# Folding the even columns of a 1024-point real transform once more on VectorE, forward and inverse

## The chip, the cores and the metric

The kernel runs on one core of one Trainium2 chip. Its time is the device time of that core in microseconds (us); lower is better, and a median over several runs is quoted. "Span" is the length of the one profiled execution.

A round is a series in which several kernels and the kernel before run in turn on one chip. The kernel before had a median of 1442.5 us (3 runs) when the prediction was made, 1442.78 us beside the changed kernel, and 1444.96, 1441.37 and 1440.81 us in the three rounds of experiments.

## The reference, cut to what matters

```python
def _A_ref(x, w_r, w_i):                    # the spectral branch
    X = jnp.fft.rfft2(x.astype(jnp.float32), axes=(-2, -1))
    X = X * (w_r + 1j * w_i)
    return jnp.fft.irfft2(X, s=(S, D), axes=(-2, -1)).astype(jnp.bfloat16)

def _B_ref(x, w1, b1, w2, b2):              # the dense branch: squared ReLU
    h = jnp.einsum("bsd,df->bsf", x, w1) + b1
    r = jnp.where(h > 0, h, 0)
    return jnp.einsum("bsf,fd->bsd", r * r, w2) + b2

g = sigmoid((x * gate_w).sum(-1, keepdims=True))
out = g * _A_ref(x, ...) + (1 - g) * _B_ref(x, ...)
# returned: out and, for a given grad_out, the gradients of all inputs of the two branches
# S = 2048, D = 1024, F = 3584, everything bfloat16
```

For output and gradient the kernel needs two real 2D transforms forward (of `x` and of the gated gradient) and two back. Each consists of 16 row tiles of 128 rows, so there are 32 forward and 32 inverse tiles. The change concerns the transform along D = 1024 inside each tile.

## The kernel before

TensorE does the dense branch in matmuls of 512 columns. Transform tiles are woven into that stream by generators: `spread` runs a step of the transform after a given number of dense steps. A forward tile is folded on VectorE, goes through eight 128-column matmuls (the part of the transform along S inside the tile, called "blocks" below), is copied to SBUF by ScalarE (`ft`), goes through eight matmuls against constant tables (the "column stage"), and is copied out of PSUM by ScalarE (`u`), with even and odd outputs interleaved.

```python
def one_s1(fb, cf, T, i, xt, kmat):                  # a forward tile
    ...                                              # uv: sum and difference of the two halves
    f = fb.tile([P, 4, Q], FDT, name="f", tag="f", bufs=2)
    a0, a1 = uv[:, :, 1:Q], uv[:, :, H - 1 : Q : -1]
    V(out=f[:, 0:2, 1:Q], in0=a0, in1=a1, op=ALU.add)
    V(out=f[:, 2:4, 1:Q], in0=a0, in1=a1, op=ALU.subtract)
    ...                                              # two small copies for the edge elements
    pk = fps.tile([P, 8, P], FP32, name="pk", tag="ps2", bufs=2)
    fl = f[:].rearrange("p a b -> p (a b)")
    for b in range(8):                               # the blocks
        mm(pk[:, b, :], lhsT=fl[:, b * P : (b + 1) * P], rhs=kmat, start=True, stop=True)
    ft = fb.tile([P, 8, P], FDT, name="ft", tag="ft", bufs=2)
    nc.scalar.copy(out=ft[:], in_=pk[:])
    pu = fps.tile([P, 2, H], FP32, name="pu", tag="ps2", bufs=2)
    column_stage(FWD, pu, ft, cf)                    # 512+257+257+255 and 4x256 columns
    u = fb.tile([P, H, 2], FDT, name="u", tag="u", bufs=2)
    nc.any.tensor_copy(out=u[:].rearrange("p j b -> p b j"), in_=pu[:])
    st(out=z_scr[T][:]..., in_=u[:]...)

FWD = (
    (4, 0, 0, H, 1), (0, 0, 0, Q + 1, 0), (1, 0, 0, Q + 1, 0), (5, 0, Q + 1, Q - 1, 2),
    (6, 1, 0, Q, 1), (7, 1, 0, Q, 2), (2, 1, Q, Q, 1), (3, 1, Q, Q, 2),
)
...
def mlp_in():                                        # the dense stage beside the forward tiles
    ...
            ph = mps.tile([P, SW], FP32, name="ph", tag="ph", bufs=2)
            for dc in range(DC):                     # eight matmuls of 512 columns
                mm(ph[:], lhsT=w1g[:, dc, fs], rhs=xT[:, dc, ss], start=(dc == 0), stop=(dc == DC - 1))
            rT = wb.tile([P, SW], BF16, name="rT", tag="rT", bufs=3)
            nc.scalar.activation(rT[:], ph[:], ACT.Relu, bias=b1col[:, fc : fc + 1])
            nc.scalar.activation(h2T[:, ss], rT[:], ACT.Square)
            pd = mps.tile([P, SW], FP32, name="pd", tag="ph", bufs=2)
            for ec in range(DC):                     # eight more
                mm(pd[:], lhsT=w2T[f2][:, ec, :], rhs=dbT[:, ec, ss], start=(ec == 0), stop=(ec == DC - 1))
            STT(out=dhT[:, ss], in0=pd[:], scalar=2.0, in1=rT[:], op0=ALU.mult, op1=ALU.mult, ...)
    ...
def fft_out():                                       # the inverse tiles
    ...
            for b in range(8):
                par, q4 = divmod(b, 4)
                mm(pk[:, b, :], lhsT=r[:, q4 * P : (q4 + 1) * P, par], rhs=ki[:], start=True, stop=True)
            rt = ...                                 # ScalarE copy, as ft above
            column_stage(INV, pu, rt, ci)
            e = fb.tile([P, 2, H], FDT, name="e", tag="e", bufs=2)
            nc.scalar.copy(out=e[:], in_=pu[:])
            ...                                      # VectorE unfolds e, result to DRAM
```

`ph` and `pd` share a tag with two buffers. So the eight matmuls of the next `ph` cannot start before the ReLU `rT` has read the last one, and ScalarE does the ReLU in order, behind the copies of the transform tile.

## Time and profile before

| | kernel before |
|---|---|
| time, median of 3 runs | 1442.5 us (1440.09 to 1443.06) |
| span of the profiled run | 1438.6 us |
| forward tiles (32) | about 83 to 433 us, beside `ph` and `pd` |
| inverse tiles (32) | about 890 to 1134 us, beside the weight gradients and the output |
| `u` copy on ScalarE, 128x1024, written at step 2 | 1304 ns |

The lines on which the bound was read stand in the prediction below. Here is one steady forward tile in the timeline of the kernel before, TensorE and ScalarE alone. The columns are start (us), duration (us), engine, line, operation, output and inputs, tile and count, and in brackets the idle time before it with what ended it.

```profile
214.33 1.17 PE L267 MATMUL pu<-cf,ft 128*128 128x512 f16 x8
...
215.34 1.24 PE L583 MATMUL ph<-xT,w1g 128*128 128x512 bf16 x5
215.54 1.31 ACT L251 CAST u<-pu 128x1024 f16<-128x1024 f32 x1 [1.07 <-PE pu L267]
...
216.42 1.89 PE L591 MATMUL pd<-dbT,w2T 128*128 128x512 bf16 x8
216.71 0.69 ACT L585 ACTIVATE rT<-ph,b1col 128x512 bf16<-128x512 f32 x1
...
218.15 1.89 PE L583 MATMUL ph<-xT,w1g 128*128 128x512 bf16 x8
```

TensorE finishes the column stage, then five matmuls of `ph`, then eight of `pd`. Meanwhile ScalarE copies `u` and then does the ReLU. The 218.15 at which TensorE writes the ReLU's buffer again is the pace of an unbroken stream: 216.42 + 8 x 0.216 = 218.15.

### The profile page before, as it was taken

The numbers are of one execution on the slowest core, as the hardware profiler recorded it, in microseconds if no ns is written. First come the engines' busy times: TensorE is split into PE (matmuls) and PEld (weight loads), VectorE is DVE, ScalarE is ACT, GpSimd is POOL, SyncE is SP. The second block draws the span as 40 slices with busy tenths as digits, with TensorE's granted clock in tenths as the row PEclk, the third lists the DMA queues.
The fourth block names the chain that finished last, engine by engine and source line by source line (L and its number), as shares of the span: only waits on it lengthen the run. The fifth ranks groups of instructions, "written<-read, shape, count | busy, mean of one in ns | idle before, by whom it ended". The sixth has DMA issues, their size and how long they took to land. (4 is left out here: it accounts for less than half of the span.)

```text
span 1438.6 us, 19451 instructions
## 1 busy us (share of the span) xinstructions
PE 1394.8 (97%) x7562; PEld 674.0 (47%) x7562; DVE 674.9 (47%) x1303; ACT 420.0 (29%) x590; POOL 299.3 (21%) x483
## 2 busy tenths in 40 slices
PE   6689999999999999999999999999999999999997
PEld 4455555555554444444444444445554444444443
DVE  2564554455444466445554534113566555652222
ACT  4245555555553322222232222334322100000000
POOL 0012222222223333333442122111110000000000
PEclk9899999999999999999999999999999999999999
DMA  7476766666669967998977678777557647563530
GB/s 234 128 235 205 218 193 204 223 216 205 191 183 255 257 200 201 187 229 189 220 146 187 143 132 188 221 205 231 194 198 228 210 147 221 177 187 96 146 95 22
DMA packets 220214, 271.57 MB, mean 189 GB/s; under 512 B 16077, under 2 KB 153307, under 8 KB 220123
## 3 DMA queue, kind: packets, MB, share of 16 engines
q1 hardware_dynamic: 184122, 151.80, 39.9%
q0 software_dynamic: 36000, 118.54, 27.9%
q8 instruction: 59, 0.97, 0.3%
q14 instruction: 33, 0.26, 0.1%
HBM read 151.77 MB, written 118.51 MB: 188 GB/s over the span
## 5 line engine op out<-in xcount | busy, mean ns | idle before, releaser
L583 PE MATMUL ph<-xT,w1g 128*128 128x512 bf16 x896 | 218.6, 382 | 1.4 <-ACT xT L493 0.9
L591 PE MATMUL pd<-dbT,w2T 128*128 128x512 bf16 x896 | 215.3, 383 | 1.6 <-DVE dbT L493 1.6
L692 PE MATMUL pw<-grp,res 128*128 128x512 bf16 x896 | 209.6, 387 | 0.0
L675 PE MATMUL pw<-dbn,grp 128*128 128x512 bf16 x896 | 198.0, 379 | 1.5 <-DVE row L639 1.5
L753 PE MATMUL acc<-w,hblk 128*128 128x512 bf16 x896 | 198.6, 379 | 0.0
L794 PE MATMUL accg<-w1Tr,hblk 128*128 128x512 bf16 x896 | 193.5, 379 | 0.0
L591 PEld LDWEIGHTS <-w2T 128*128 128x128 bf16 x896 | 87.4, 99 | 109.1 <-issue 5.1
L585 ACT ACTIVATE rT<-ph,b1col 128x512 bf16<-128x512 f32 x112 | 77.0, 688 | 207.9 <-PE ph L583 159.7
L794 PEld LDWEIGHTS <-hblk 128*128 128x128 bf16 x896 | 87.7, 98 | 105.7
L675 PEld LDWEIGHTS <-grp 128*128 128x128 bf16 x896 | 87.1, 98 | 105.8 <-issue 2.4
L692 PEld LDWEIGHTS <-res 128*128 128x128 bf16 x896 | 85.0, 96 | 109.0
L753 PEld LDWEIGHTS <-hblk 128*128 128x128 bf16 x896 | 87.0, 98 | 98.6
L583 PEld LDWEIGHTS <-w1g 128*128 128x128 bf16 x896 | 85.3, 98 | 86.6 <-issue 4.5
L592 DVE SCALAR_TENSOR_TENSOR dhT<-pd,rT 128x512 bf16<-128x512 f32 x112 | 75.3, 673 | 104.5 <-PE pd L591 60.9
L604 DVE STREAM_TRANSPOSE stg<-h2T 128x512 int32<-128x512 int32 x56 | 39.8, 711 | 130.2 <-ACT h2T L586 130.2
L679 ACT CAST wo<-pw 128x512 bf16<-128x512 f32 x56 | 32.8, 586 | 165.7 <-PE pw L675 152.3
L697 ACT CAST wo<-pw 128x512 bf16<-128x512 f32 x56 | 32.9, 587 | 142.0 <-PE pw L692 132.2
L687 POOL DMA_DIRECT2D out_dram<-wo x112 | 56.3, 516 | 81.9 <-ACT wo L679 61.4
L795 DVE TENSOR_TENSOR gxo<-accg,g 128x512 bf16<-128x512 f32 x32 | 22.1, 691 | 107.6 <-PE accg L794 107.4
L306 DVE CAST x<-px 128x1024 f16<-128x1024 f32 x16 | 19.6, 1224 | 111.5 <-PE px L305 111.5
L461 DVE TENSOR_TENSOR tt<-e 128x512 f16<-128x512 f16 x32 | 13.6, 425 | 124.2 <-ACT e L459 123.5
L586 ACT ACTIVATE h2T<-rT 128x512 bf16<-128x512 bf16 x112 | 70.5, 629 | 3.4
(169 smaller groups left out, 1488.6 us busy)
## 6 DMA issues: line engine op xcount, KB each, us to landing
h_scr<-stg POOLq DMA_DIRECT2D x28, 512.0 KB, 6.1
dh_scr<-stg POOLq DMA_DIRECT2D x28, 512.0 KB, 7.4
h2T_scr<-h2T POOLq DMA_DIRECT2D x28, 512.0 KB, 4.9
dhT_scr<-dhT POOLq DMA_DIRECT2D x28, 512.0 KB, 6.6
grp<-h_scr SPq DMA_DIRECT2D x112, 128.0 KB, 5.3
grp<-dh_scr SPq DMA_DIRECT2D x112, 128.0 KB, 4.6
hblk<-h2T_scr SPq DMA_DIRECT2D x8, 1792.0 KB, 9.1
hblk<-dhT_scr SPq DMA_DIRECT2D x8, 1792.0 KB, 8.9
```

The lines of the kernel that those rows point to most:

```text
L583: mm(ph[:], lhsT=w1g[:, dc, fs], rhs=xT[:, dc, ss], start=(dc == 0), stop=(dc == DC - 1))
L585: nc.scalar.activation(rT[:], ph[:], ACT.Relu, bias=b1col[:, fc : fc + 1])
L586: nc.scalar.activation(h2T[:, ss], rT[:], ACT.Square)
L591: mm(pd[:], lhsT=w2T[f2][:, ec, :], rhs=dbT[:, ec, ss], start=(ec == 0), stop=(ec == DC - 1))
L592: STT(out=dhT[:, ss], in0=pd[:], scalar=2.0, in1=rT[:], op0=ALU.mult, op1=ALU.mult, accum_out=gb1part[:, fc, sb : sb + 1],)
L604: nc.vector.transpose(out=stg[k_, sb][:, :, f2, :], in_=src[:, cols2].bitcast(I32).rearrange("p (b i) -> p b i", i=32),)
L675: mm(pw[:], lhsT=cur[:, t // 2, 2 * fb_ * P + t % 2 : 2 * (fb_ + 1) * P : 2], rhs=dbn[:, t, hf * H : (hf + 1) * H], start=(t == 0), stop=( ...
L687: st(out=dst[q], in_=wo[32 * q : 32 * (q + 1), :])
L692: mm(pw[:], lhsT=xr[t][:, d_ * P : (d_ + 1) * P], rhs=cur[:, t // 2, t % 2 :: 2], start=(t == 0), stop=(t == NT - 1),)
L697: nc.scalar.copy(out=wo[:].rearrange("p (q a j) -> p a q j", q=4, j=32), in_=pw[:].rearrange("p (a q j) -> p a q j", q=4, j=32),)
L753: mm(acc[:], lhsT=cur[:, fc, t2::2], rhs=w2[:, fc, cs], start=(fc == 0), stop=(fc == FC - 1))
L794: mm(acc[:], lhsT=cur[:, fc, t2::2], rhs=w1T[:, fc, cs], start=(fc == 0), stop=(fc == FC - 1))
```

## The change

The even-numbered outputs of the transform can be split once more into those divisible by four and the others. For that VectorE forms sums and differences of mirrored halves, forward before the blocks and inverse after the column stage. In exchange the four even matmuls of a column stage shrink from 512, 257, 257 and 255 columns to 256, 129, 128 and 128. In the changed kernel `u` collects four groups of outputs, one for each remainder on division by four, so its copy, which restores the natural order, writes runs of 256 elements at a step of four instead of two. The inverse reads its stationary blocks at a step of four.

```diff
-        f = fb.tile([P, 4, Q], FDT, name="f", tag="f", bufs=2)
+        f = fb.tile([P, 6, Q], FDT, name="f", tag="f", bufs=2)
         ...
+        b0, b1 = f[:, 0:3:2, 1:P], f[:, 0:3:2, Q - 1 : P : -1]
+        V(out=f[:, 4:6, 1:P], in0=b0, in1=b1, op=ALU.add)
+        V(out=f[:, 4:6, P + 1 : Q], in0=b0, in1=b1, op=ALU.subtract)
+        V(out=f[:, 4, 0:1], in0=uv[:, 0, 0:1], in1=uv[:, 0, Q : Q + 1], op=ALU.add)
+        V(out=f[:, 4, P : P + 1], in0=uv[:, 0, 0:1], in1=uv[:, 0, Q : Q + 1], op=ALU.subtract)
+        nc.scalar.copy(out=f[:, 5, P::-P], in_=f[:, 0:3:2, P])
         ...
-        nc.any.tensor_copy(out=u[:].rearrange("p j b -> p b j"), in_=pu[:])
+        nc.any.tensor_copy(
+            out=u[:].rearrange("p (i h) b -> p b h i", h=2), in_=pu[:].rearrange("p b (h i) -> p b h i", h=2)
+        )
         ...
     FWD = (
-        (4, 0, 0, H, 1), (0, 0, 0, Q + 1, 0), (1, 0, 0, Q + 1, 0), (5, 0, Q + 1, Q - 1, 2),
-        (6, 1, 0, Q, 1), (7, 1, 0, Q, 2), (2, 1, Q, Q, 1), (3, 1, Q, Q, 2),
+        (0, 0, 2 * P, 0, 1), (0, 0, P + 1, 0, 2), (0, 2 * P, P, 0, 3), (0, 3 * P, P, 0, 3),
+        (1, 0, 2 * P, P, 1), (1, 0, 2 * P, P, 2), (1, P, 2 * P, P, 1), (1, P, 2 * P, P, 2),
     )
         ...
-                    mm(pk[:, b, :], lhsT=r[:, q4 * P : (q4 + 1) * P, par], rhs=ki[:], start=True, stop=True)
+                    mm(pk[:, b, :], lhsT=rf[:, im * H + l_ : (im + 1) * H : 4], rhs=ki[:], start=True, stop=True)
         ...
+                ev = fb.tile([P, 2, Q], FDT, name="ev", tag="ev", bufs=2)
+                A, B = (e[:, 0, o : o + Q].rearrange("p (c d) -> p c d", c=2) for o in (0, Q))
+                V(out=ev[:, :, 0:P], in0=A, in1=B, op=ALU.add)
+                evf = ev[:].rearrange("p c d -> p (c d)")
+                V(out=evf[:, Q:P:-1], in0=A[:, 0, :], in1=B[:, 0, :], op=ALU.subtract)
+                V(out=evf[:, 2 * Q - 1 : Q + P : -1], in0=B[:, 1, 1:], in1=A[:, 1, 1:], op=ALU.subtract)
+                nc.vector.tensor_copy(out=ev[:, :, P : P + 1], in_=e[:, 0, P::Q].rearrange("p (c o) -> p c o", o=1))
         ... # cut: the constant tables cf and ci in their new order, INV, the unfolding that reads ev
```

More of the change, by code (lines that the diff above doesn't have):

```diff
@@ L64, in build_consts @@
     w = lambda l, d: tp * ((l[None, :] * d[:, None]) % D) / D
-    le, lo = np.arange(0, D // 2 + 1, 2), np.arange(1, D // 2, 2)
-    lei = le[1:-1]
+    l4, l42 = np.arange(0, D // 2 + 1, 4), np.arange(2, D // 2, 4)
+    lo = np.concatenate([np.arange(1, D // 2, 4), np.arange(3, D // 2, 4)])
     d0, d1 = np.arange(P), np.arange(P, 2 * P)
-    dz = d0.copy()
-    dz[0] = Q
-    even = np.zeros((P, 2 * Q))
-    even[:, Q + 1 :] = -np.sin(w(lei, d0))
-    even[0, : Q + 1] = np.cos(w(le, np.array([Q])))[0]
+    dz, dh = d0.copy(), d0.copy()
+    dz[0], dh[0] = Q, P
+    blk_n = np.concatenate([np.zeros((P, P + 1)), -np.sin(w(l4[1:-1], d0))], axis=1)
+    blk_n[0, : P + 1] = np.cos(w(l4, np.array([P])))[0]
     parts = [
-        even,
-        np.cos(w(le, d0)), np.cos(w(le, d1)), -np.sin(w(lei, d1)),
+        blk_n, np.cos(w(l4, d0)), np.cos(w(l42, d0)), -np.sin(w(l42, dh)),
         np.cos(w(lo, d0)), np.cos(w(lo, d1)), -np.sin(w(lo, dz)), -np.sin(w(lo, d1)),
@@ L78, in build_consts @@
     c["cf"] = np.concatenate(parts, axis=1).astype(FDT_NP)
-    de, ds = np.arange(Q + 1), np.arange(1, Q)
+    v = lambda l, d: tp * ((l[:, None] * d[None, :]) % D) / D
+    cof = lambda l: np.where((l == 0) | (l == 2 * Q), 1.0, 2.0)[:, None]
     dq = np.arange(Q)
@@ L83, in build_consts @@
     dzq[0] = Q
-    l0e, l1e = np.arange(0, Q, 2), np.arange(Q, 2 * Q, 2)
-    l0o, l1o = np.arange(1, Q, 2), np.arange(Q + 1, 2 * Q, 2)
-    v = lambda l, d: tp * ((l[:, None] * d[None, :]) % D) / D
-    cof = lambda l: np.where((l == 0) | (l == 2 * Q), 1.0, 2.0)[:, None]
-    ev = np.zeros((P, 2 * Q))
-    ev[1:, Q + 1 :] = -2.0 * np.sin(v(l0e[1:], ds))
-    ev[0, : Q + 1] = np.cos(np.pi * de)
+    m4, m42 = np.arange(0, D // 2, 4), np.arange(2, D // 2, 4)
+    m1, m3 = np.arange(1, D // 2, 4), np.arange(3, D // 2, 4)
+    da = np.arange(P + 1)
+    ev = np.concatenate([np.zeros((P, P + 1)), -2.0 * np.sin(v(m4, da[1:-1]))], axis=1)
+    ev[0] = 0.0
+    ev[0, : P + 1] = np.cos(np.pi * da)
     parts = [
-        ev,
-        cof(l0e) * np.cos(v(l0e, de)), cof(l1e) * np.cos(v(l1e, de)), -2.0 * np.sin(v(l1e, ds)),
-        2.0 * np.cos(v(l0o, dq)), 2.0 * np.cos(v(l1o, dq)), -2.0 * np.sin(v(l0o, dzq)), -2.0 * np.sin(v(l1o, dzq)),
+        ev, cof(m4) * np.cos(v(m4, da)), 2.0 * np.cos(v(m42, d0)), -2.0 * np.sin(v(m42, dh)),
+        2.0 * np.cos(v(m1, dq)), 2.0 * np.cos(v(m3, dq)), -2.0 * np.sin(v(m1, dzq)), -2.0 * np.sin(v(m3, dzq)),
     ]
@@ L239, in one_s1 @@
         V(out=f[:, 2:4, 1:Q], in0=a0, in1=a1, op=ALU.subtract)
-        nc.scalar.copy(out=f[:, 0::3, 0:1], in_=uv[:, :, 0:1])
-        nc.scalar.copy(out=f[:, 2:0:-1, 0:1], in_=uv[:, :, Q : Q + 1])
+        nc.scalar.copy(out=f[:, 3, 0:1], in_=uv[:, 1, 0:1])
+        nc.scalar.copy(out=f[:, 1, 0:1], in_=uv[:, 1, Q : Q + 1])
+        b0, b1 = f[:, 0:3:2, 1:P], f[:, 0:3:2, Q - 1 : P : -1]
[4 more added lines that the diff above has]
+        nc.scalar.copy(out=f[:, 5, P::-P], in_=f[:, 0:3:2, P])
         pk = fps.tile([P, 8, P], FP32, name="pk", tag="ps2", bufs=2)
-        fl = f[:].rearrange("p a b -> p (a b)")
-        for b in range(8):
-            mm(pk[:, b, :], lhsT=fl[:, b * P : (b + 1) * P], rhs=kmat, start=True, stop=True)
+        for b, (row, o) in enumerate(((5, P), (4, 0), (4, P), (5, 0), (3, 0), (3, P), (1, 0), (1, P))):
+            mm(pk[:, b, :], lhsT=f[:, row, o : o + P], rhs=kmat, start=True, stop=True)
         ft = fb.tile([P, 8, P], FDT, name="ft", tag="ft", bufs=2)
@@ L250, in one_s1 @@
         u = fb.tile([P, H, 2], FDT, name="u", tag="u", bufs=2)
-        nc.any.tensor_copy(out=u[:].rearrange("p j b -> p b j"), in_=pu[:])
+        nc.any.tensor_copy(
+            out=u[:].rearrange("p (i h) b -> p b h i", h=2), in_=pu[:].rearrange("p b (h i) -> p b h i", h=2)
+        )
         st(out=z_scr[T][:].rearrange("c (p i) l -> i (c p) l", i=S2)[i], in_=u[:].rearrange("p j b -> p (j b)"))
     FWD = (
-        (4, 0, 0, H, 1), (0, 0, 0, Q + 1, 0), (1, 0, 0, Q + 1, 0), (5, 0, Q + 1, Q - 1, 2),
-        (6, 1, 0, Q, 1), (7, 1, 0, Q, 2), (2, 1, Q, Q, 1), (3, 1, Q, Q, 2),
-    )
-    INV = (
-        (2, 0, 0, H, 1), (0, 0, 0, Q + 1, 0), (1, 0, 0, Q + 1, 0), (3, 0, Q + 1, Q - 1, 2),
-        (4, 1, 0, Q, 1), (5, 1, 0, Q, 2), (6, 1, Q, Q, 1), (7, 1, Q, Q, 2),
-    )
+        (0, 0, 2 * P, 0, 1), (0, 0, P + 1, 0, 2), (0, 2 * P, P, 0, 3), (0, 3 * P, P, 0, 3),
+        (1, 0, 2 * P, P, 1), (1, 0, 2 * P, P, 2), (1, P, 2 * P, P, 1), (1, P, 2 * P, P, 2),
+    )
+    INV = FWD[:4] + ((1, 0, Q, 0, 1), (1, 0, Q, 0, 2), (1, Q, Q, 0, 1), (1, Q, Q, 0, 2))
     def column_stage(table, pu, ft, mat):
         o = 0
-        for (b, bank, lo, n, f_) in table:
+        for b, (bank, lo, n, skip, f_) in enumerate(table):
+            out = pu[:, bank, lo : lo + n]
+            if skip:
+                out = pu[:, bank, :].rearrange("p (h c i) -> p c h i", h=2, c=2)[:, lo // P]
             mm(
-                pu[:, bank, lo : lo + n], lhsT=ft[:, b, :], rhs=mat[:, o : o + n],
+                out, lhsT=ft[:, b, :], rhs=mat[:, o : o + n],
                 start=bool(f_ & 1), stop=bool(f_ & 2), skip_group_check=True,
@@ L450, in fft_out @@
                 pk = fps.tile([P, 8, P], FP32, name="pki", tag="ps2", bufs=2)
-                for b in range(8):
-                    par, q4 = divmod(b, 4)
-                    mm(pk[:, b, :], lhsT=r[:, q4 * P : (q4 + 1) * P, par], rhs=ki[:], start=True, stop=True)
+                rf = r[:].rearrange("p j b -> p (j b)")
+                for b, (im, l_) in enumerate(((1, 0), (0, 0), (0, 2), (1, 2), (0, 1), (0, 3), (1, 1), (1, 3))):
+                    mm(pk[:, b, :], lhsT=rf[:, im * H + l_ : (im + 1) * H : 4], rhs=ki[:], start=True, stop=True)
                 rt = fb.tile([P, 8, P], FDT, name="rt", tag="rt", bufs=2)
@@ L459, in fft_out @@
                 nc.scalar.copy(out=e[:], in_=pu[:])
+                ev = fb.tile([P, 2, Q], FDT, name="ev", tag="ev", bufs=2)
[5 more added lines that the diff above has]
+                nc.vector.tensor_copy(out=ev[:, :, P : P + 1], in_=e[:, 0, P::Q].rearrange("p (c o) -> p c o", o=1))
                 tt = fb.tile([P, 2, 2, Q], FDT, name="tt", tag="tt", bufs=2)
-                V(out=tt[:, 0].rearrange("p a b -> p (a b)"), in0=e[:, 0, :], in1=e[:, 1, :], op=ALU.add)
-                V(out=tt[:, 1].rearrange("p a b -> p (a b)"), in0=e[:, 0, :], in1=e[:, 1, :], op=ALU.subtract)
+                V(out=tt[:, 0].rearrange("p a b -> p (a b)"), in0=evf, in1=e[:, 1, :], op=ALU.add)
+                V(out=tt[:, 1].rearrange("p a b -> p (a b)"), in0=evf, in1=e[:, 1, :], op=ALU.subtract)
                 yo = fb.tile([P, D], FDT, name="yo", tag="yo", bufs=2)
```

## The prediction

> **What bounds the kernel now.** I read the page's busy shares first, then its forty slices, then the windows view by stage, then the timeline of TensorE, and last the groups by line.
>
> ```profile
> PE 1394.8 (97%) x7562; PEld 674.0 (47%) x7562; DVE 674.9 (47%) x1303; ACT 420.0 (29%) x590; POOL 299.3 (21%) x483
> ...
> PE   6689999999999999999999999999999999999997
> ...
> PEclk9899999999999999999999999999999999999999
> ```
>
> TensorE is busy from the fourth slice to the last at full clock; only the first three slices (about 108 us) hold gaps. The windows view, cut at the stage borders (us, PE, PEld, DVE, ACT, POOL busy, then clock, DMA share, GB/s), says the same with numbers:
>
> ```profile
> 0.00:108.00 108.00, 79.24 (x655) 48.24 (x656) 52.18 (x100) 41.19 (x57) 10.05 (x17) 0.95 0.64 199
> 108.00:440.00 332.00, 331.36 (x2014) 170.62 (x2013) 165.16 (x390) 171.88 (x270) 92.52 (x126) 1.00 0.67 204
> 440.00:900.00 460.00, 455.34 (x2204) 205.63 (x2203) 229.21 (x364) 129.22 (x176) 147.37 (x250) 1.00 0.83 196
> 900.00:1134.00 234.00, 232.32 (x1326) 115.78 (x1325) 99.03 (x253) 76.91 (x89) 33.95 (x63) 1.00 0.68 211
> ```
>
> The changed forward tiles run in 83 to 433 us, the inverse ones in about 890 to 1134 us: nearly all in the second and fourth window, where TensorE idles 0.6 of 332 and 1.7 of 234 us while VectorE is busy 50% and 42%. So time taken off TensorE's queue there comes off the end, and time put on VectorE there is free unless it delays something TensorE waits for. Busy TensorE is not peak TensorE (ends are modelled), so I take the pace from starts in the timeline of TensorE (start, length, what):
>
> ```profile
> 1098.71 1.24 PE L753 MATMUL acc<-w,hblk 128*128 128x512 bf16 x5
> 1099.79 0.61 PE L453 MATMUL pki<-ki,r 128*128 128x128 f16 x8
> 1100.23 1.24 PE L753 MATMUL acc<-w,hblk 128*128 128x512 bf16 x5
> 1101.56 1.17 PE L267 MATMUL pui<-ci,rt 128*128 128x512 f16 x8
> 1102.57 5.12 PE L753 MATMUL acc<-w,hblk 128*128 128x512 bf16 x23
> ```
>
> Five matmuls of 512 columns take 1099.79 - 1098.71 = 1.08 us, 216 ns each. Eight of 128 columns take 0.44 us, 55 ns each: at this size the weight load does not yet set the pace. The eight of one column stage (512+257+257+255+4x256 = 2305 columns) take 1.01 us. And the five fillers before the column stage take 1.33 us instead of 1.08: about 0.25 us in which TensorE waits for the ScalarE copy of the eight blocks, hidden inside "busy".
>
> **What the Trainium skill says.** "TensorE: Matmul & The Clock Gate", section Back-to-back issue gap, gives N/2.4 + 2.5 ns warm: 215.8 ns at 512 and 55.8 at 128. The trace agrees (216 and 55), and does not show the 81 ns that the same section names for pairs of load and matmul at 128. The same page, Weight-path perf modes, has the fast weight load allowed for column steps from -1,023 to 1,024 elements. This bears on the inverse, whose stationary operand goes from step 2 to step 4; the trace shows step 2 at 55 ns, no run yet shows step 4. "Advanced Engine Details and Errata", Memory Cachelines, says that SBUF needs at least two hits on a 16-byte line for full speed: step 4 of fp16 has exactly two. For writes the trace already disagrees: ScalarE's copy at step 2 costs 1304 ns, the packed one 1012. "VectorE: DVE Perf Modes", tier table, gives 16-bit tensor_tensor in SBUF two elements a cycle; 425 ns at 512 and 682 at 1024 (0.50 ns per element) agree.
>
> **The change part by part.**
>
> Removed from TensorE. Per tile, the even columns' 512+257+257+255 = 1281 columns become 256+129+128+128 = 641; the odd half keeps 4x256, forward and inverse keep eight matmuls each, and the eight block transforms before stay. From 216 = a + 512b and 55 = a + 128b: b = 0.419 ns, a = 1.3 ns. So 640 x 0.419 = 268 ns per tile, and 64 tiles (32 forward, 32 inverse) make **17.2 us**. Nothing is given back in count. Of this all but the startup tile lies on the path that sets the end.
>
> Added to VectorE. From the groups:
>
> ```profile
> L238 DVE TENSOR_TENSOR f<-uv 128x510 f16<-128x510 f16 x32 | 13.2, 414 | 0.0
> L292 DVE TENSOR_TENSOR pm<-z 128x1024 f16<-128x1024 f16 x14 | 9.6, 682 | 0.0
> L372 DVE TENSOR_TENSOR pc<-v 128x1 f16<-128x1 f16 x14 | 2.2, 154 | 0.0
> L376 DVE COPY pc<-v 128x2 f16<-128x2 f16 x2 | 0.3, 171 | 0.0
> ```
>
> L238 reads one input backwards and is still fast, so slope (682-414)/514 = 0.52 ns, fixed 148 ns. Forward: two of 254 elements at 280, two of one at 154: 868 ns. Inverse: 256 elements at 282, 128 and 127 at 215, a copy of two at 171: 883 ns. Together (868+883) x 32 = **56 us**, VectorE 675 to about 731 us. In the forward window it goes from 50% to some 58%. All beside TensorE.
>
> Added to ScalarE. One more tiny copy per forward tile (204 ns, 6.5 us in all), and the copy of the result to SBUF now writes at step 4 instead of 2:
>
> ```profile
> L247 ACT CAST ft<-pk 128x1024 f16<-128x1024 f32 x32 | 32.4, 1012 | 28.7 <-PE pk L245 28.7
> L251 ACT CAST u<-pu 128x1024 f16<-128x1024 f32 x32 | 41.7, 1304 | 36.8 <-PE pu L267 36.8
> ```
>
> I estimate 1.3 to 1.9 us for it, by adding the step from packed to stride 2 (0.29 us) none, one or two times; ScalarE in the forward window goes from 52% to at most 60%. Behind it in ScalarE's queue stands the ReLU that frees a PSUM buffer of the main matmuls. In one tile that I followed it ran from 216.71 to 217.40 and its buffer is written again at 218.15, so 0.75 us is free: more than my upper estimate adds.
>
> Moved. The instruction order of the built change has the same steady pattern: the same 2560 columns of filler behind the block transforms in all but a few tiles, before and after, so the wait of about 0.25 us per tile stays. One difference is at the start. Before, two forward tiles ran in the holes of the startup; now one does, as the longer VectorE chain makes the second tile late, and it falls into the full stretch:
>
> ```profile
> 85.23 0.61 PE L245 MATMUL pk<-kf,f 128*128 128x128 f16 x8
> 87.65 0.39 PE L267 MATMUL pu<-cf,ft 128*128 128x512 f16 x1 [1.82 <-ACT ft L247]
> ...
> 88.77 0.95 PE L267 MATMUL pu<-cf,ft 128*128 128x257 f16 x7
> 89.56 0.38 PE L245 MATMUL pk<-kf,f 128*128 128x128 f16 x4
> 89.89 1.89 PE L591 MATMUL pd<-dbT,w2T 128*128 128x512 bf16 x8
> ```
>
> That tile costs 0.44 (blocks) + 0.74 (new column stage) + 0.25 (wait) later, and 0.22 for the half set of blocks at 89.56: 1.65 us. The matmul at 89.89 can start perhaps 0.4 us sooner, as it needs the last transposed block, which stood in the queue behind the 1.82 us wait. Net **+1.2 us**. The constant tables shrink from 2305 to 1665 columns (0.16 MB less each); the DMA engines are 64 to 83% busy and nothing on TensorE's path waits for these two, so I count zero.
>
> Sum: 1442.5 - 17.2 + 1.2 = 1426.5; I add half a microsecond for small waits and say **1427 us**, a ratio of 0.989.
>
> **The rivals.** (a) Slow weights at step 4: if the load of the inverse blocks left the fast path, 256 matmuls would go from 55 to perhaps 108 ns, +14 us, and the time would be about 1440. For it: exactly two hits per line is the edge. Against it: step 2 costs nothing at all. One in ten. (b) ScalarE's stride-4 copy is dearer than estimated, over 2 us: the ReLU comes late, and TensorE waits some tenths in each of 32 tiles, up to 10 us; time about 1435. For it: stride 2 already costs 29%. Against it: 0.75 us of slack. One in seven. (c) VectorE becomes the bound: 12 more operations stand in line with the evictions of the main matmuls, in order. At 58% mean, with PSUM buffers freed about 1 us ahead, I expect a few tenths here and there; at worst 5 us. In the inverse stretch before the end of the transforms VectorE was busy 50 of 80 us and gets to about 60, with four accumulators in rotation. (d) The gain is larger: if the shorter column stage closes with the copy, or the startup shifts well, 1421.
>
> **Range and chances.** The columns are certain, worth 17 us; the three losses above are each unlikely, and the startup can move by 2 or 3 us either way, also because two short stretches there run at half clock (0.95 in the first window). The runs of before spread by 3 us. So 1421 to 1434 eight times in ten. Two per cent is 28.9 us: faster than that needs nearly twice the columns that leave, slower needs several rivals at once. Chances: 0.01 faster, 0.97 within, 0.02 slower.
>
> **What would show it.** Right: column stage start to start from 1.01 to about 0.74 us; the even-column matmuls of 128 at about 55 to 58 ns; TensorE's gaps no larger; VectorE up 55 us without a share over 65% in a stage; the blocks of the inverse still 0.44 us for eight; ScalarE's u copy under 1.9 us. Wrong: inverse blocks at 0.8 us for eight (rival a); idle time or gaps before the main matmuls of the first stage released by ScalarE (b) or VectorE (c); the first full-pace main matmul after the startup later than 91 us.

## The result, and the profile after

| | before | after |
|---|---|---|
| median | 1442.78 us (4 runs, 1440.09 to 1443.5) | 1450.3 us (4 runs, 1448.43 to 1452.79) |
| span of the profiled run | 1438.6 us | 1450.2 us |
| ratio, 95% interval | | 1.0057 (1.0033 to 1.0080) |

The changed kernel is correct. It is about half a per cent slower where one per cent faster was expected, and lies outside the predicted range.

These are the page's line of busy shares after and three of its groups (line, engine, operation, output and inputs, count, then busy us and mean ns of one, then idle before it and what ended it):

```profile
PE 1379.4 (95%) x7419; PEld 668.1 (46%) x7562; DVE 709.6 (49%) x1559; ACT 457.4 (32%) x622; POOL 299.9 (21%) x483
...
L595 PE MATMUL ph<-xT,w1g 128*128 128x512 bf16 x866 | 214.9, 382 | 10.8 <-ACT rT L597 5.8
L603 PE MATMUL pd<-dbT,w2T 128*128 128x512 bf16 x870 | 214.0, 385 | 11.2 <-DVE w2T L570 6.5
...
L254 ACT CAST u<-pu 128x1024 f16<-128x1024 f32 x32 | 78.3, 2447 | 17.9 <-PE pu L272 17.9
```

TensorE fell from 97% to 95% busy. The `u` copy went from 1304 to 2447 ns. `ph` and `pd` now wait, for the ReLU on ScalarE and for a copy on VectorE. This trace lost 143 of 7562 matmul records, but no weight load; so the sums below are taken from the starts of weight loads. The windows view after (us, then PE, PEld, DVE, ACT, POOL busy, clock, DMA share, GB/s):

```profile
0.00:108.00 108.00, 76.34 (x619) 46.19 (x628) 51.36 (x106) 40.32 (x55) 8.87 (x15) 0.87 0.62 192
108.00:440.00 332.00, 314.73 (x1909) 161.28 (x1944) 175.51 (x502) 199.46 (x292) 89.25 (x122) 1.00 0.66 197
...
900.00:1134.00 234.00, 230.75 (x1322) 115.19 (x1346) 113.64 (x364) 77.72 (x91) 38.06 (x69) 1.00 0.74 224
```

In the forward stage TensorE, which was busy for all but 0.6 of 332 us, shows 17 us without work (part of it may be lost records). ScalarE went from 171.88 to 199.46 us, VectorE only from 165.16 to 175.51. The inverse stage has no such hole. The first window ran at a clock of 0.87 instead of 0.95: more of the startup at half clock.

TensorE's waits in the changed kernel, 108 to 440 us (who waits for whom, us in total, times, longest us). For the kernel before this list is empty:

```profile
PE pd L603 <- DVE w2T L570: 6.5, 9, 0.7
PE ph L595 <- ACT rT L597: 5.8, 16, 0.6
```

And the timeline, with the end of one tile and the tile that answers to the one shown of before (from 223.28):

```profile
203.28 0.69 ACT L597 ACTIVATE rT<-ph,b1col 128x512 bf16<-128x512 f32 x1
...
204.67 0.71 DVE L616 STREAM_TRANSPOSE stg<-h2T 128x512 int32<-128x512 int32 x1 [3.22 <-ACT h2T L598]
...
205.89 0.69 DVE L570 COPY w2T<-ptw 128x1024 bf16<-128x1024 bf16 x1
...
206.63 1.90 PE L603 MATMUL pd<-dbT,w2T 128*128 128x512 bf16 x8 [0.72 <-DVE w2T L570]
...
223.28 0.91 PE L272 MATMUL pu<-cf,ft 128*128 128x256 f16 x8
...
224.03 1.24 PE L595 MATMUL ph<-xT,w1g 128*128 128x512 bf16 x5
224.23 2.46 ACT L254 CAST u<-pu 128x1024 f16<-128x1024 f32 x1 [0.81 <-PE pu L272]
...
225.11 1.89 PE L603 MATMUL pd<-dbT,w2T 128*128 128x512 bf16 x8
...
226.50 0.70 ACT L597 ACTIVATE rT<-ph,b1col 128x512 bf16<-128x512 f32 x1
...
227.25 1.89 PE L595 MATMUL ph<-xT,w1g 128*128 128x512 bf16 x8 [0.25 <-ACT rT L597]
```

The column stage takes 224.03 - 223.28 = 0.75 us, as predicted, instead of 1.01. The copy takes 2.46 us, so the ReLU runs from 226.50 to 227.20. TensorE could go on at 225.11 + 1.73 = 226.84 and goes on at 227.25: 0.41 us late. The first four lines show how the lateness spreads. After the ReLU at 203.28 comes the square `h2T`, for which VectorE has waited 3.22 us when it starts to transpose it at 204.67. In VectorE's queue `dhT` and then the copy `w2T` stand behind it, and TensorE waits another 0.72 us for `w2T`, which stands ready at 206.58.

**Where the time went.** Both traces have the same order of main (not transform) weight loads, so I compared the moments at which the same load was issued. The table gives how far the profiled run lies behind that of the kernel before (negative: ahead), in us, with times counted from the start of each span. This and the next table are my own sums from the traces.

| place (time in the kernel before) | after | e1 | e2 | e7 (before, once more) |
|---|---|---|---|---|
| 93 us, startup done | +2.0 | -2.6 | +2.8 | +0.1 |
| 124 us | +4.9 | -1.2 | +3.2 | +0.1 |
| 450 us, forward tiles done | +16.8 | -10.2 | +21.9 | +0.2 |
| 652 us | +16.8 | -10.2 | +21.9 | +0.2 |
| 716 us | +20.0 | -6.7 | +25.2 | +3.8 |
| 878 us, before the inverse tiles | +20.0 | -6.7 | +25.2 | +3.8 |
| 1162 us, after them, and to the end | +11.6 | -15.1 | +25.3 | +3.9 |

The inverse half gives 20.0 - 11.6 = 8.4 us. The forward half, which should give as much, loses 12 us between 124 and 450 us. The 3 us near 680 us also appear in a second profile of the kernel before, so they are not shown to be the change's. The 2.0 us at 93 us are explained below, with the startup.

For 28 of the forward tiles, between the same two weight loads, the second table sums the times from one weight load to the next by which pair they are (us):

| from load to load | before | after | e1 | e2 | e4 |
|---|---|---|---|---|---|
| all | 304.0 | 315.9 | 295.2 | 322.4 | 299.9 |
| inside the column stage | 22.2 | 14.8 | 14.8 | 22.2 | 14.8 |
| inside runs of w1 blocks (mostly `ph`) | 99.1 | 111.0 | 99.2 | 110.1 | 99.2 |
| from w1 to the transposed w2 (to `pd`) | 18.0 | 23.8 | 16.1 | 23.8 | 18.1 |
| inside runs of w2 (`pd`) | 103.5 | 105.2 | 104.1 | 105.1 | 106.7 |

The column stage saved 7.4 us, which is 266 ns a tile. The three rows below it lost 11.9 + 5.8 + 1.7 = 19.4 us, 0.69 us a tile. Together that is the +11.9 us of the first row.

### The profile page after: what moved, and what is told of

It reads as the page before. It is cut to its first block, busy times and chain, and to the rows that moved or that the text cites. A ratio compares the mean times of both kernels' runs of the same rounds, so it can differ in the third digit from the quotient of the medians.

```text
span 1450.2 us, 19521 instructions
## 1 busy us (share of the span) xinstructions
PE 1379.4 (95%) x7419; PEld 668.1 (46%) x7562; DVE 709.6 (49%) x1559; ACT 457.4 (32%) x622; POOL 299.9 (21%) x483
## 5 line engine op out<-in xcount | busy, mean ns | idle before, releaser
L595 PE MATMUL ph<-xT,w1g 128*128 128x512 bf16 x866 | 214.9, 382 | 10.8 <-ACT rT L597 5.8
L603 PEld LDWEIGHTS <-w2T 128*128 128x128 bf16 x896 | 87.9, 99 | 120.2 <-issue 11.6
L254 ACT CAST u<-pu 128x1024 f16<-128x1024 f32 x32 | 78.3, 2447 | 17.9 <-PE pu L272 17.9
L311 DVE CAST x<-px 128x1024 f16<-128x1024 f32 x16 | 19.6, 1224 | 113.7 <-PE px L310 113.7
```

Of the source, the lines that this page charges most:

```text
L254: nc.any.tensor_copy(out=u[:].rearrange("p (i h) b -> p b h i", h=2), in_=pu[:].rearrange("p b (h i) -> p b h i", h=2))
```

## The experiments

My theory (A) was that the longer `u` copy alone holds up ScalarE, and through the ReLU TensorE. The rivals: (B) the operations added on VectorE delay its evictions and the `w2T` copy, for which TensorE waits too; (C) other order, tables or startup. Kernels e1 to e4 ran in one round, e5, e6, e7 and e9 in a second, e10 to e12 in a third; each result is of 4 runs against 7 of the kernel before. All give correct results except e2.

| | us, median (range) | ratio to before (95%) | `u` copy ns |
|---|---|---|---|
| e1: after, packed write | 1428.73 (1425.31-1432.49) | 0.9891 (0.9867-0.9914) | 1012 |
| e2: before, step-4 write | 1463.02 (1462.14-1465.78) | 1.0125 (1.0107-1.0144) | 2441 |
| e3: inverse half alone | 1429.28 (1428.8-1430.9) | 0.9896 (0.988-0.9911) | 1304 |
| e4: after, copy on VectorE | 1437.2 (1434.47-1437.64) | 0.9945 (0.9927-0.9962) | 2439 |
| e5: after, step-2 write | 1429.5 (1427.33-1430.82) | 0.9911 (0.9895-0.9928) | 1306 |
| e6: before, packed write | 1439.26 (1437.96-1440.0) | 0.9979 (0.9964-0.9995) | 1012 |
| e7: before, unchanged | 1440.44 (1438.71-1444.38) | 0.9992 (0.997-1.0014) | 1304 |
| e9: e1, column stage a tile later | 1414.47 (1414.04-1418.79) | 0.9817 (0.9793-0.984) | 1019 |
| e10: e6, column stage a tile later | 1427.14 (1425.12-1428.5) | 0.9905 (0.989-0.992) | 1013 |
| e11: forward half alone, packed write | 1433.33 (1432.66-1433.52) | 0.9948 (0.9932-0.9965) | 1012 |
| e12: e3, table padded to old size | 1432.22 (1430.95-1433.7) | 0.9942 (0.9927-0.9957) | 1304 |

### e1_packed_u: the changed kernel, the copy writing without a step

```diff
-        nc.any.tensor_copy(
-            out=u[:].rearrange("p (i h) b -> p b h i", h=2), in_=pu[:].rearrange("p b (h i) -> p b h i", h=2)
+        nc.scalar.copy(
+            out=u[:].rearrange("p (i h) b -> p i h b", h=2), in_=pu[:].rearrange("p b (h i) -> p i h b", h=2)
         )
```

The same elements go to the same places, but the loop runs in the order of the output: it writes element after element, and jumps in PSUM on the reading side instead.

> The whole change, but the ScalarE copy of a forward tile's result walks in the order of its output, so that it writes packed and reads PSUM scattered. Theory A (the write at step 4 made this copy 2447 ns, and it holds up the ReLU behind it): the copy falls to 1.0 to 1.4 us, the stalls of the forward stretch go, and the time is 1428 us (1425 to 1432). Rival B (the four more VectorE operations per tile delay the evictions): the copy may get shorter, but the time stays at 1445 to 1451. Rival C (it is the number of dimensions or the scattered PSUM read that costs): the copy stays at 2.4 us and the time at 1448 to 1453.

Measured: 1428.73 us, 0.9891 of before, and 1.7% below the changed kernel by the two ratios (0.9891 / 1.0057 = 0.983). The view of the tile `u` (minimum, median, maximum of its durations in ns) and the forward stage in the windows view:

```profile
L254 ACT CAST u<-pu x32: 1003/1012/1012, 82.4 to 422.8; 128x1024 f16<-128x1024 f32 x32
```

```profile
108.00:440.00 332.00, 331.37 (x2064) 172.36 (x2063) 182.31 (x512) 171.89 (x303) 95.27 (x129) 1.00 0.70 214
```

The copy is shorter than even the kernel before had it. TensorE is full again, while VectorE does all the added work (182 of 332 us). The waits of TensorE are gone from the waits view of this stage, that for `w2T` included. So (A) holds and (B) falls: with the added VectorE work in place, the view lists no wait. (C) falls too, as order, tables and startup code are those of the changed kernel; and the copy, which reads in jumps and is written with as many dimensions as the slow one, takes 1012 ns, so neither of these made it slow. The stage is 8.8 us shorter than before over 28 tiles, 7.4 of them by columns.

### e2_before_step4: the kernel before, with the copy of the changed one

```diff
-        nc.any.tensor_copy(out=u[:].rearrange("p j b -> p b j"), in_=pu[:])
+        nc.scalar.copy(
+            out=u[:].rearrange("p (i h) b -> p b h i", h=2), in_=pu[:].rearrange("p b (h i) -> p b h i", h=2)
+        )
```

The values land in the wrong places; the work is the same otherwise.

> The kernel before, with nothing changed but the order in which this copy writes: step 4, as in the change (the forward columns land in a wrong order, so the outputs of the transform are wrong on purpose). Theory A: the copy takes about 2.45 us instead of 1.30, TensorE waits about 0.75 us per tile, and the time rises by some 23 us to 1466 (1458 to 1470). Rival B: VectorE's work is as before, so the time stays within 4 us of 1443.

Measured: 1463.02 us, 1.0125, the copy 2441 ns. Its waits from 108 to 440 us:

```profile
PE pd L593 <- DVE w2T L560: 5.7, 8, 0.7
...
PE ph L585 <- ACT rT L587: 3.8, 8, 0.6
```

These are the waits of the changed kernel, without any fold. Over the 28 tiles this copy alone costs 322.4 - 304.0 = 18.4 us, 0.66 us a tile; the loss in the changed kernel was 0.69. Adding the saved columns, +18.4 - 7.4 = +11.0 us, comes within 1 us of the changed kernel's +11.9. The wait for `w2T` on VectorE is thus a consequence of the copy on ScalarE, not of VectorE's own work.

### e4_u_on_vector: the same copy on VectorE

```diff
-        nc.any.tensor_copy(
+        nc.vector.tensor_copy(
             out=u[:].rearrange("p (i h) b -> p b h i", h=2), in_=pu[:].rearrange("p b (h i) -> p b h i", h=2)
         )
```

> The whole change, with this copy on VectorE, still at step 4. Theory A, in the form that ScalarE's queue is the one that matters: ScalarE is free of it, and if VectorE writes step 4 without a penalty (about 1.22 us, as its other copies of 1024 from PSUM) the time is 1428 to 1436. If VectorE pays the same penalty (over 2 us), its queue holds up the other eviction and the time is 1445 to 1460.

Measured: 1437.2 us, 0.9945. The copy's group on the page, and the wait of TensorE that is left from 108 to 440 us:

```profile
L254 DVE CAST u<-pu 128x1024 f16<-128x1024 f32 x32 | 78.0, 2439 | 1.4 <-PE pu L272 1.4
```

```profile
PE pd L603 <- DVE dhT L604: 2.0, 7, 0.4
```

I had named two branches, and it took neither: the penalty is there on VectorE as well (2439 ns; VectorE's packed evictions of the same size, `x` from `px`, take 1224), yet the kernel is faster than before. What counts is who stands behind the copy. On VectorE it costs 299.9 - 304.0 + 7.4 = 3.3 us over the 28 tiles, 0.12 us a tile against 0.69.

### e5_step2_u: the changed kernel, the copy at step two

```diff
-        nc.any.tensor_copy(
-            out=u[:].rearrange("p (i h) b -> p b h i", h=2), in_=pu[:].rearrange("p b (h i) -> p b h i", h=2)
+        nc.scalar.copy(
+            out=u[:].rearrange("p (i h) b -> p b i h", h=2), in_=pu[:].rearrange("p b (h i) -> p b i h", h=2)
```

> The whole change, this copy in a third order, so that it writes at step 2 as the kernel before did, still reading PSUM scattered. If the byte step of the write sets its length: 1.30 us as before, between packed (1011 ns) and step 4 (2447 ns), and the stalls stay away: 1427 to 1433 us, within 3 us of the packed one. If any step above packed made the ReLU late in this schedule: 1435 or more.

Measured: 1429.5 us, 0.9911, the copy 1306 ns at the median. The step of the write sets the duration: 1012 ns packed, 1306 at step two, 2447 at step four, for the same 1024 elements a partition. From one to two it costs 0.29 us, from two to four 1.14 us. The 28 tiles take 296.7 us, 7.3 less than before: the columns and nothing else, since this copy costs what that of before costs. For the same reason this run prices the whole fold most directly: 0.9911 is 12.8 us (10.4 to 15.1).

### e6_before_packed: the kernel before, the copy packed

```diff
-        nc.any.tensor_copy(out=u[:].rearrange("p j b -> p b j"), in_=pu[:])
+        nc.scalar.copy(out=u[:], in_=pu[:].rearrange("p b j -> p j b"))
```

> The kernel before with this copy packed, nothing else: the fair partner of the packed change. The copy takes 1.01 instead of 1.30 us. Theory A with slack (0.3 us of ScalarE off the path is worth nothing): same as before within 2 us. If the kernel before already lost something to this copy: 2 to 6 us faster, and then part of the packed change's gain belongs to the copy and not to the fold.

Measured: 1439.26 us, 0.9979. By the ratio the kernel before had lost 3 us to its step of two (the interval allows 0.7 to 5.2), and 1.3 us over the 28 tiles of the traces (304.0 - 302.7). The fold therefore has to be compared with this kernel where its copy is packed.

### e7_before_again: the kernel before, unchanged

There is no edit. The run shows how far two profiles of one kernel differ.

> The kernel before unchanged, with a profile: what two sets of runs of one kernel differ by on one chip. Expected: ratio 1.000 within 0.003, and a profile in which TensorE's wait near 680 us (1.7 us in the first profile, 3 us in three others) may come out otherwise. If it is 0.995 or less, the 7 us by which the inverse half beat its arithmetic are of this size and not the change's.

Measured: 1440.44 us, 0.9992. Its profiled execution fell 3.6 us behind the first one near 680 us (first table), where the traces of e7 and of the changed kernel have a wait of TensorE for ScalarE's copy `x` of over 3 us and 3.4 us at half clock. The first profile of before shows 1.7 us of that wait and no half clock. So single profiles may not be compared there.

### e3_inverse_only: only the inverse half of the change

The edit takes the inverse part of the diff above (`ci`, `INV`, the blocks at step four, `ev`) and leaves the forward part as before.

> Only the inverse half of the change. Theory A: the inverse gains what was predicted for it, 32 tiles of 268 ns = 8.6 us, so 1434 us (1432 to 1437). If stationary operands at step 4 or the longer VectorE chain cost something there: 1438 or more.

Measured: 1429.28 us, 0.9896, better than expected: some 15 us of gain where 8.6 were worked out. Its trace shows 8.4 us between 878 and 1162 us; the 2.6 us more that it gains lie outside the inverse tiles, in the startup and near 680 us. The round may have part in the rest: the kernel before was 4 us slower there than in the other two. That is not shown.

### e12_inverse_padded: the same, with the table at its old size

```diff
+    parts.append(np.zeros((P, 640)))
     c["ci"] = np.concatenate(parts, axis=1).astype(FDT_NP)
```

> Only the inverse half, and its constant table filled up with 640 columns of zeros to the old size, which are loaded and never used. The inverse half beat its arithmetic by 6 us, and its instructions are those of the kernel before up to 890 us. If the size of the table in memory (where later tensors lie, or the load itself) is why: the time goes back to 1433 or 1435 us. If not: it stays at 1429.

Measured: 1432.22 us, between the two branches; 0.9942, that is 8.4 us. This is the arithmetic of the columns. Against e3 the medians differ by 3 us, with the table's size as the only difference. But the two ran in different rounds, and single runs of one kernel differ as much, so that the table's size is the cause stays likely at best, and open.

### e11_forward_only: only the forward half, the copy packed

The edit takes the forward part of the diff and e1's copy, and leaves the inverse as before.

> Only the forward half of the change, with the packed copy. The forward fold alone: 32 tiles of 268 ns less 1 us of startup, 7.5 us under the packed kernel before, so 1432 us (1428 to 1436). If VectorE's longer chain cost something: 1437 or more.

Measured: 1433.33 us, 0.9948. Against e6, which has the same copy, that is 0.9948 / 0.9979 = 0.9969, about 4.5 us, where the columns give 8.6; the two intervals together leave some 3 us of doubt. In its trace the steady tiles do give it: from 124 to 450 us it gains 9.0 us on the kernel before, 1.3 of them by the packed copy (e6). But at 93 us it lies 2.2 us behind, and at 124 us, after the tile that left the startup, 3.5 us.

### e9_early_blocks: e1, with each column stage issued one tile later

```diff
         nc.scalar.copy(out=ft[:], in_=pk[:])
+        yield
         pu = fps.tile([P, 2, H], FP32, name="pu", tag="ps2", bufs=2)
         ...
-                one_s1(f1, cf, T, i, src, km[:])
+                half = one_s1(f1, cf, T, i, src, km[:])
+                next(half)
+                for _ in late:
+                    pass
+                late = half
                 yield
+        for _ in late:
+            pass
         ... # the same for the inverse tiles
```

A tile's blocks are now followed at once by the column stage of the tile before, whose `ft` has long been copied. This takes away the wait for the copy of the blocks, which the prediction had seen inside "busy".

> The packed change, and each tile's column stage issued one tile later, behind the next tile's block transforms, so that its weights are long there. Predicted in the text: about 0.25 us of waiting per tile, 64 tiles, hidden in TensorE's busy time. If so the time falls by some 16 us from the packed one, to 1413 (1409 to 1418). If the wait is not one for the ScalarE copy: same as the packed one.

Measured: 1414.47 us, 0.9817: the best kernel, faster than both. Its windows view of the two stages and its timeline of TensorE in one tile:

```profile
110.00:440.00 330.00, 330.00 (x2088) 177.02 (x2087) 185.72 (x518) 172.80 (x309) 96.62 (x131) 1.00 0.72 217
...
900.00:1130.00 230.00, 230.00 (x1359) 119.35 (x1358) 127.56 (x395) 69.32 (x82) 34.15 (x63) 1.00 0.71 221
```

```profile
220.01 0.61 PE L248 MATMUL pk<-kf,f 128*128 128x128 f16 x8
220.46 0.90 PE L273 MATMUL pu<-cf,ft 128*128 128x256 f16 x8
221.19 1.89 PE L614 MATMUL ph<-xT,w1g 128*128 128x512 bf16 x8
```

The column stage starts 0.45 us after the blocks, which is their own time, and takes 0.73 us. Over the 28 tiles of the traces it is 295.2 - 289.8 = 5.4 us shorter than e1, 0.19 us a tile. e1's median is 14.3 us longer, but it comes from another round; by the ratios, 0.9817 / 0.9891 = 0.9925, it is 10.8 us, or 0.17 us for each of 64 tiles. That much was waiting, although TensorE was "busy" 331.37 of 332 us in e1 too.

### e10_before_early: e6 with the same order

The edit is that of e9 on the kernel before with e6's copy, without the fold.

> The kernel before with the packed copy and with each column stage one tile later, without the fold. If the wait per tile and the fold add up: 1439 minus 16 = 1423 us (1420 to 1427), and the fold is then worth 9 us between this and the folded kernel with both. If the later column stage only helps where the column stage is short: 1435 or more.

Measured: 1427.14 us, 0.9905, a little slower than expected; the gain over e6 is 12 us by the medians and 10.7 by the ratios (0.9905 / 0.9979). It also prices the fold without that wait around it: 0.9817 / 0.9905 = 0.9911, about 12.7 us, with some 4 us of doubt as the two ran in different rounds. e5 gave 12.8, and from the halves it comes out alike: 4.5 us (e11 over e6) and 8.4 us (e12).

## Why the prediction was wrong

It was right that the time would stay within 2%, and wrong on the direction: 1450.3 us instead of 1427, outside 1421 to 1434. By its own steps:

- **Columns off TensorE: right.** 266 ns a tile forward, where 268 were worked out; the inverse tiles gave 8.4 us, where half of 17.2 was expected.
- **VectorE: right in each operation, immaterial in the sum.** The new operations took 284 and 283 ns (254 elements), 154 and 153 (one), 291, 222 and 221, and 165. Their durations add up to the predicted 56 us, but VectorE's busy time rose by 35, since in the trace operations in a row overlap: two of 0.15 us start 0.07 us apart. Rival (c) counted 12 more operations; there are eight, four forward and four inverse (1559 - 1303 = 256 = 32 x 8). With them in place TensorE's list of waits is empty (e1), so rival (c) falls.
- **Inverse blocks at step four: right.** Start to start they took 56 ns as before; rival (a) did not happen. The weight load itself did get longer, 113 ns instead of 98 (tile `r`, median), but that stayed hidden behind the matmuls.
- **The copy on ScalarE: the step that failed.** In its words: "I estimate 1.3 to 1.9 us for it, by adding the step from packed to stride 2 (0.29 us) none, one or two times", against 0.75 us of slack, "more than my upper estimate adds". It measured 2447 ns, 1.14 us more than before (e5, e2). The slack in the followed tile had been read well: 0.75 minus the 1.11 us by which the ReLU ends later after the column stage's copy begins is a lateness of 0.36 us, and 0.41 were seen. The profile held ScalarE copies of this size at step two (`u` at 1304 ns, `xT` at 1308) and none above; a straight line from packed through step two was no basis. Nor did the slack of one tile hold for all. In an earlier tile of the kernel before, `w2T` stood ready at 198.38 us and the `pd` behind it started at 198.43, while the unbroken stream would have had it at 196.54 + 1.73 = 198.27: on that path nothing was to spare, and even step two instead of packed costs 1.3 to 1.5 us over the 28 tiles (e6, and e5 against e1).
- **Rival (b): the right mechanism, mis-sized.** It was given one chance in seven, "some tenths" a tile and "up to 10 us". The loss was 0.69 us a tile, 19.4 us over 28 tiles. Not foreseen was that the late ReLU also holds up the square behind it, its transposition on VectorE, and behind that the copy `w2T`; that accounts for 6.5 us of TensorE's listed waits.
- **The startup: right in its two terms, but not in the clock.** The moved tile cost 1.3 to 1.5 us between 93 and 124 us in e1, e5 and e11 (2.8 in the changed kernel, with its stall), where the prediction had 1.65. The 0.4 us it credited for an earlier start is seen in e1, which was 2.1 us ahead of the kernel before at 85 us and began the `pd` in question at 87.33 instead of 89.89, 2.6 us ahead. In the changed kernel a stretch at half clock hides it: from 87.2 to 94.0 us the granted clock was 0.50, against 1.00 in the kernel before, and at 93 us it lay 2.0 us behind. Five of the six profiles with the forward fold have such a stretch there (all but e1), but so have two of the seven without it (e2, e10), so that the fold brings it on is not shown; why the clock halves was not tested. By e11 over e6 the forward half lost about 4 us to all this (with the doubt of 3 us named there), not 1.2.
- **The wait of 0.25 us a tile that "stays": right,** and worth about 11 us by the ratios when taken away (e9 over e1, e10 over e6). The 0.25 was read in an inverse tile; by the starts in the kernel before it is 0.24 us there at the median, and 0.19 in a forward tile.

With the copy written packed (e1) the ratio is 0.9891, the predicted one. That is partly luck: the packed copy brings about 3 us of its own (e6), and that round's kernel before was 2 to 4 us slower than in the others. The fold itself is worth some 13 us (12.8 by e5, 12.7 by e9 over e10) where the prediction had 16.

## What to carry to other kernels

When a change rearranges data, price the new access step of every copy around it from a measured row of that very step, and if there is none, measure it before relying on slack; and let the copy out of PSUM write packed and jump on its reading side, which was free here. Then ask what stands behind the longer operation in its engine's queue: the same 2.44 us cost 0.69 us a tile ahead of the ReLU on ScalarE, and 0.12 on VectorE. A full "busy" line can still hide waits: compare starts with the pace of an unbroken stream.

## What the Trainium skill lacked or had wrong

- "Advanced Engine Details and Errata", section Memory Cachelines, asks for at least two hits on a 16-byte SBUF line. Step four of 16-bit elements has exactly two. For weight reads the matmuls kept their pace (56 ns each, as at step two), though the load itself went from 98 to 113 ns. For writes it misleads: 1012 ns packed, 1306 at step two, 2447 at step four on ScalarE. The section has no cost by step of a write.
- The same section says that non-contiguous access to PSUM slows matmuls a good deal, and nothing of engines that read it. ScalarE read 1024 fp32 elements in jumps of 256 and 512 in the same 1012 ns that a packed copy takes (e1).
- "VectorE: DVE Perf Modes", tier table, sorts by type and memory only, and gives no time for a write at a step. An eviction from PSUM took VectorE 1224 ns packed and 2439 at an output step of four (e4).
- "TensorE: Matmul & The Clock Gate", section Back-to-back issue gap, gives 81 ns for pairs of load and matmul at 128 columns. At full clock the kernels here ran them at 55 to 56 ns. Nor is the same sentence's 131 ns at 512 columns seen: they ran at 216.
